# Joining the attention visits of units 8 to 11 on TensorE in a fused chunk-attention and MoE kernel

## The chip, the cores and the metric

The kernel runs on one core of one Trainium2 chip. The metric is the device time of one execution in microseconds (us). Before the change its median over 8 runs is 288.11 us, from 287.54 to 290.14.

## What is computed

`q`, `k` and `v` have shape (8, 8, 576, 64): 8 batches, 8 heads, 576 positions, 64 values per head, all in fp32. Attention is done inside chunks of 64 positions, with no mask. Its result, put together over the heads, is the 4608 x 512 input of a two-layer network with a gated activation.

```python
scores = (1/sqrt(64)) * q_c @ k_c.T          # per chunk of 64 positions, per head
attn   = softmax(scores)
x      = (attn @ v_c)                         # -> 4608 x 512, heads side by side
h      = x @ w_in                             # 512 -> 2048
out    = (h * sigmoid(beta * h)) @ w_out      # 2048 -> 512
```

## The kernel before, in words

**Tiles.** The 4608 tokens are cut into 18 units of 256 tokens. Two units make a block of 512 tokens, so there are 9 blocks, 0 to 8. A unit holds two halves of 128 tokens, called `s` = 0 and 1.

**Attention of one unit.** POOL (GpSimd) loads q and k in fp16 (L99 from unit 8 on, L105 before) and v into one large resident tile `vbig` (L113). From unit 8 on (`XU = 8`, L73) the q and k of a unit are turned by two DMA transposes that SP issues (`emit_T`, L152), first k and then q; before unit 8 VectorE does it. `emit_sc` then issues 32 matmuls of 64x64 (L225) that put the scores of the unit into the PSUM tile `s` (two banks), and one ScalarE exponential (L231) that writes `et`. `emit_pv` issues 32 matmuls of 64x65 (L266): for each half 16 products of `et` and v, with a column of ones that gives the row sums. `emit_norm` (L285, L287) takes reciprocals and multiplies on VectorE and leaves the half in `x16`. `emit_xt_dma` (L318) has SP issue the DMA transpose of that half into `xt`, the moving operand of the block's first layer.

**The network of one block.** `emit_m(j, m)` is one of 16 slices of the first layer: 4 matmuls of 128x128 by 512 (L329) into one PSUM bank `hps`, a tanh on ScalarE (L339) and a VectorE instruction (L343) that forms the gated slice. `emit_t(j, t)` is one of 4 tiles of 128 tokens of the second layer: 16 matmuls (L361), issued in two halves of 8, then a ScalarE copy out of PSUM (L371) and an output DMA on SP (L373). `hps`, `ops` and the tiles `y` (below) share four PSUM banks, the pool `ps_p`. The tiles `x` and `s` have two banks each.

**Order.** The order on each engine is the order in which the code emits, since the schedule is written out by hand. Blocks 0 to 2 are written out line by line. From block 3 on (L563) each block is a list of items sorted by a position between 0 and 1: the 16 slices `m` of block j, the 8 half tiles `t` of block j-1, and the attention of the two units of block j+1. An attention item between two items of the network makes TensorE leave its 128x128 matmuls for a set of 64x64 ones; I call that a visit.

**Two ways to place attention.** Units below `MU` = 12 (L74) get separate visits from `att_items` (L558): one for the scores (`sc`), and one for the second product (`pv`) 0.40 of a half block later. Their `pv` writes the halves 0 and 1 into the PSUM tiles `x` and `s`. From unit 12 on there is one visit per unit, a "hop" (L586): `pv` of unit u, right behind it the scores of unit u+1, then the DMA transposes of unit u+2, then the norms. A hop must leave the tile `s` to the scores, so its half 1, which is done first, goes into two `ps_p` banks as `y0` and `y1`, and half 0 into `x`. Hops stand at 0.22 and 0.68 of a block. At the end of block 4 a visit for the scores of unit 12 leads over to the hops.

**Queues.** SP issues output DMAs and all DMA transposes in order. POOL issues the loads in order. The load of a unit's q needs a buffer of the pool `qk` (4 deep), which comes free when the DMA transpose of the unit four before has landed. `emit_T(u)` also emits the loads up to unit u+4 (L164), except for units 6, 7 and 8.

Of the kernel before, what the change touches and what calls it, by code (L numbers as in the profile page):

```python
# [15 lines left out]
def kernel(  # L16
# [18 lines left out]
    NU = NT // UNIT  # L35
# [35 lines left out]
    blocks = [(u, 2) for u in range(0, NU, 2)]  # L71
    NB = len(blocks)
    XU = 8  # L73
    MU = 12  # L74
    unit_block = {}
    for j, (u0, n) in enumerate(blocks):
        for u in range(u0, u0 + n):
# [47 lines left out]
    def loads_to(u):  # L125
        while nxt[0] <= min(u, NU - 1):
            load_unit(nxt[0])
            nxt[0] += 1
# [16 lines left out]
    def emit_T(u, which=("kT", "qT")):  # L145
        for nm in which:
            src, dst = {"kT": (k_t, kT), "qT": (q_t, qT)}[nm]
            a = src.pop(u)
            t = qt_p.tile([128, H, CH, 2], FP16, tag=nm, name=nm)
            dst[u] = t  # L150
            if u >= XU:
                nc.sync.dma_start_transpose(  # L152
                    out=t.rearrange("p h s e -> p (h s e)").rearrange("p (j t) -> p j t", t=128),
                    in_=a.rearrange("p h r d -> p (h r d)"),
                )
                continue
            nc.vector.transpose(
                out=t.rearrange("p h s e -> p (h s e)").bitcast(FP32).rearrange(
                    "p (h i r) -> p h r i", h=H, r=2),
                in_=a.rearrange("p h r d -> p (h r d)").bitcast(FP32).rearrange(  # L160
                    "p (h r i) -> p h r i", h=H, r=2),
            )
        if which[-1] == "qT" and u not in (6, 7, 8):
            loads_to(u + 4)  # L164
# [48 lines left out]
    def emit_ex(u):  # L213
        ex_t[u].pop(0)()

    def emit_sc(u, split=False, later=False):
        qt, kt = qT.pop(u), kT.pop(u)
        sc = ps_s.tile([128, 2, H, CH], FP32, tag="s", name="sc")
        if u >= XU:
            qx, kx = (t.rearrange("p h s e -> p (h s e)").rearrange("p (j c t) -> p j c t", j=H, c=2)  # L220
                      for t in (qt, kt))
            for jj in range(H):
                for par in range(2):
                    for c in range(2):
                        nc.tensor.matmul(  # L225
                            out=sc[64 * c:64 * c + 64, par, jj, :],
                            lhsT=kx[64 * par:64 * par + 64, jj, c, :],
                            rhs=qx[64 * par:64 * par + 64, jj, c, :],
                        )
            et = et_p.tile([128, 2, H, CH], FP16, tag="et", name="et")  # L230
            nc.scalar.activation(out=et, in_=sc, func=ACTF.Exp, scale=scale)  # L231
            et_t[u] = et
            return
        for h in range(H):
            for e in range(2):
                for c in range(4):
                    p0, o0 = 32 * c, 64 * (c % 2)
                    nc.tensor.matmul(  # L238
                        out=sc[o0:o0 + 64, c // 2, h, :],
                        lhsT=kt[p0:p0 + 32, h, :, e],  # L240
                        rhs=qt[p0:p0 + 32, h, :, e],
                        start=(e == 0),
                        stop=(e == 1),
                    )
        et = et_p.tile([128, 2, H, CH], FP16, tag="et", name="et")
        ex_t[u] = [
            lambda s=s: nc.scalar.activation(out=et[:, s], in_=sc[:, s], func=ACTF.Exp, scale=scale)  # L247
            for s in ([0, 1] if split or later else [slice(0, 2)])
        ]
        et_t[u] = et  # L250
        while ex_t[u] and not later:
            emit_ex(u)

    def emit_pv(u, where=("x", "s")):
        et = et_t.pop(u)
        for s in (1, 0) if u >= MU else (0, 1):
            i = 2 * u + s
            if where[s] == "p":
                x = [ps_p.tile([128, 4, 128], FP32, tag="p", name=f"y{r}") for r in range(2)]
            else:  # L260
                pool = {"x": ps_x, "s": ps_s}[where[s]]
                x = [pool.tile([128, 2, 4, 128], FP32, tag=where[s], name="x")]
            for g in range(4):
                for r in range(2):
                    for c in range(2):
                        nc.tensor.matmul(  # L266
                            out=(x[0][64 * c:64 * c + 64, r, g, 0:D + 1] if len(x) == 1 else
                                 x[r][64 * c:64 * c + 64, g, 0:D + 1]),
                            lhsT=(et[64 * r:64 * r + 64, s, 4 * c + g, :] if u < XU else
                                  et[64 * r:64 * r + 64, g % 2, 4 * s + 2 * c + g // 2, :]),  # L270
                            rhs=vbig[64 * r:64 * r + 64, i, 4 * c + g, 0:D + 1],
                        )
            x_t[u, s] = x

    def emit_norms(u):
        for s in (1, 0) if u >= MU else (0, 1):
            emit_norm(u, s)
            emit_xt_dma(u, s)

    def emit_norm(u, s):  # L280
        x = x_t.pop((u, s))
        rd = rd_p.tile([128, 2, 4, 1], FP32, tag="rd", name="rd")
        x16 = x_p.tile([128, 2, 4, D], FP16, tag="x16", name="x16")
        for r, z in [(slice(0, 2), x[0])] if len(x) == 1 else list(enumerate(x)):
            nc.vector.reciprocal(out=rd[:, r], in_=z[..., D:D + 1])  # L285
            o = x16[:, r]
            nc.vector.tensor_tensor(  # L287
                out=o, in0=z[..., 0:D], in1=rd[:, r].to_broadcast(list(o.shape)), op=ALU.mult
            )
        x16_t[u, s] = x16  # L290

    def xt_at(u, s):
        j, o = unit_block[u]
        if j not in xt_t:
            xt_t[j] = xt_p.tile([128, 4, 4, 128], FP16, tag="xt", name="xt")
        return xt_t[j][:, 2 * o + s]
# [19 lines left out]
    def emit_xt_dma(u, s):  # L316
        xf = x16_t.pop((u, s)).rearrange("p r h d -> p (r h d)")
        nc.sync.dma_start_transpose(out=xt_at(u, s), in_=xf)  # L318
# [75 lines left out]
    with tc.manual_schedule():  # L394
# [74 lines left out]
        for i in range(16):  # L469
# [11 lines left out]
            if i == 15:  # L481
                a0, v0 = emit_m(1, 0, 0, 256, True)
# [46 lines left out]
        for m in range(KFF):  # L529
# [22 lines left out]
            if m == 7:  # L552
# [1 line left out]
                emit_gate(7)  # L554
                emit_xt_dma(7, 1)
                loads_to(11)

        def att_items(u, a0, w):  # L558
            return [(a0, 2, ("sc", u)), (a0 + 0.40 * w, 3, ("pv", u)),
                    (a0 + 0.40 * w, 4, ("norm", u, 0)), (a0 + 0.40 * w, 5, ("norm", u, 1)),  # L560
                    (a0 + 0.10 * w, 3, ("T", u + 1))]

        for j in range(3, NB):  # L563
            items = [(0.02 + 0.98 * m / KFF, 0, ("m", m)) for m in range(KFF)]
            for t in range(4):
                for hf in range(2):
                    items.append((0.98 * (t + 0.5 * hf) / 4, 1, ("t", t, hf)))
            if 2 * j + 2 < MU:
                for i in range(2):
                    items += att_items(2 * j + 2 + i, 0.03 + 0.43 * i, 0.43)  # L570
                if 2 * j + 4 == MU:
                    items += [(0.89, 2, ("sc", MU)), (0.90, 3, ("T", MU + 1))]
            elif j + 1 < NB:
                for i in range(2):
                    items.append((0.22 + 0.46 * i, 2, ("hop", 2 * j + 2 + i)))
            items.sort(key=lambda it: it[:2])
            for _, _, it in items:
                if it[0] == "m":
                    emit_m(j, it[1])
                elif it[0] == "t":  # L580
                    emit_t(j - 1, it[1], 8 * it[2], 8 * it[2] + 8)
                elif it[0] == "sc":
                    emit_sc(it[1])
                elif it[0] == "pv":
                    emit_pv(it[1])
                elif it[0] == "hop":  # L586
                    emit_pv(it[1], ("x", "p" if it[1] + 1 < NU else "s"))
                    if it[1] + 1 < NU:
                        emit_sc(it[1] + 1)
                    if it[1] + 2 < NU:  # L590
                        emit_T(it[1] + 2)
                    emit_norms(it[1])
                elif it[0] == "norm":
                    emit_norm(it[1], it[2])
                    emit_xt_dma(it[1], it[2])
                elif it[1] < NU:
                    emit_T(it[1])
        for t in range(3):
# [48 lines left out]
```

## Time and profile before

| what | value |
|---|---|
| median of 8 runs | 288.11 us |
| the profiled execution, its own time | 288.08 us |
| its span, first to last instruction | 286.2 us |
| PE busy | 278.9 us, 97% of the span |
| VectorE, ScalarE, POOL busy | 143.2, 146.5, 95.7 us |
| matmuls of L329 | 612, 136.3 us busy |
| matmuls of L361 | 560, 131.1 us busy |
| matmuls of L225 (scores, units 8 to 17) | 320, 32 in a visit |
| matmuls of L266 into `x` and into `y` | 464 and 112 recorded |
| DMA moved | 37.40 MB, mean 131 GB/s |
| granted TensorE clock | 1.000 |

The profile is of one execution. The span leaves 1.9 us of its own time outside. PE is TensorE's matmuls, PEld its weight loads, DVE VectorE, ACT ScalarE, SP the engine that issues DMAs. A line such as L329 is a line of the kernel. The chain of work follows from the last instruction back through what released each step; a stretch of it is a start, a length, and the instructions in it.

### The profile page before, as it was taken

To read this page: it belongs to the slowest core of one execution; us is meant where nothing else is said; L and a number is where in the kernel's file an instruction comes from. 1 tells how busy PE (TensorE), PEld (TensorE's weight loads), DVE (VectorE), ACT (ScalarE), POOL (GpSimd) and SP (SyncE) were. 2 spreads that over 40 slices of the span, in tenths; PEclk is the share of its full clock that TensorE was granted. 3 is DMA by queue.
4 is the path that set the end of the run, shared out by engine and by line. 5 is a ranking of instruction groups with operands and counts; after the bars stand their busy time and mean duration, and the time that the engine had idled before them with its cause. 6 is when DMAs were issued, how large, how long until landed. Compare 5 with 4: busy or idle time off the path is not lost.

```text
span 286.2 us, 6667 instructions
## 1 busy us (share of the span) xinstructions
PE 278.9 (97%) x2779; PEld 136.1 (48%) x2779; DVE 143.2 (50%) x264; ACT 146.5 (51%) x223; POOL 95.7 (33%) x125
## 2 busy tenths in 40 slices
PE   6889999999999999999999999999999999999995
PEld 3564456544544444444444444444444444444444
DVE  3678444776558553535353636354545544333301
ACT  4378228773557545454545555454546444444411
POOL 8753678488073991253643610000000000000000
PEclk9999999999999999999999999999999999999999
DMA  8999999999999999999999999364451212010012
GB/s 193 176 197 206 179 180 213 208 166 152 206 112 167 182 176 166 159 142 139 167 142 168 127 152 157 101 90 95 58 129 39 73 39 73 37 39 37 37 73 76
DMA packets 141085, 37.40 MB, mean 131 GB/s; under 512 B 128000, under 2 KB 136576, under 8 KB 141056
## 3 DMA queue, kind: packets, MB, share of 16 engines
q0 software_dynamic: 99136, 17.83, 80.5%
q1 hardware_dynamic: 41776, 19.09, 33.7%
q8 instruction: 22, 0.36, 0.5%
q10 hardware_dynamic: 144, 0.07, 0.1%
q14 instruction: 7, 0.06, 0.0%
HBM read 36.71 MB, written 9.44 MB: 161 GB/s over the span
## 4 chain that ended last, share of the span: by engine, by line
PE 94%; DMA 3%; ACT 1%; issue 1%; DVE 0%; POOL 0%; DVEq 0%; POOLq 0%
PE hps L329 44%; PE ops L361 43%; DMA h<-in_k_dram 3%; PE x L266 2%; PE sc L238 1%; PE ops L603 1%; PE sc L225 1%; ACT xt L304 1%; PE y L266 1%; PE xp L303 0%; PE sc L198 0%; ACT et L208 0%; POOL h L401 0%; PE warm L381 0%; PE xp L311 0%
## 5 line engine op out<-in xcount | busy, mean ns | idle before, releaser
L343 DVE SCALAR_TENSOR_TENSOR gt<-sg,hps 128x512 f16<-128x512 f32 (+1 forms) x153 | 99.2, 655 | 104.7 <-ACT sg L339 104.3
L339 ACT ACTIVATE sg<-hps,beta 128x512 f32<-128x512 f32 (+1 forms) x153 | 100.4, 663 | 71.9 <-PE hps L329 70.3
L329 PE MATMUL hps<-xt,win 128*128 128x512 f16 (+1 forms) x612 | 136.3, 367 | 0.8 <-ACT xt L304 0.7
L361 PE MATMUL ops<-wout,gt 128*128 128x512 f16 x560 | 131.1, 379 | 0.0
L329 PEld LDWEIGHTS <-win 128*128 128x128 f16 x612 | 58.4, 98 | 62.9 <-issue 0.9
L361 PEld LDWEIGHTS <-gt 128*128 128x128 f16 x560 | 53.8, 98 | 63.3
L371 ACT ACTIVATE osb<-ops 128x512 f32<-128x512 f32 x35 | 20.9, 598 | 42.6 <-PE ops L361 42.6
L113 POOL DMA_DIRECT2D vbig<-in_v_dram x40 | 34.1, 874 | 9.9 <-DMA wout<-in_moe_w_out_dram 3.7
L99 POOL DMA_DIRECT2D qu<-in_q_dram x22 | 18.7, 863 | 36.8 <-DMA qT<-qu 34.5
L287 DVE TENSOR_TENSOR x<-x,rd 128x512 f16<-128x512 f32 x29 | 20.1, 692 | 1.1
L99 POOL DMA_DIRECT2D ku<-in_k_dram x22 | 18.9, 880 | 0.2 <-issue 0.2
L285 DVE RECIPROCAL rd<-x 128x8 f32<-128x8 f32 x29 | 5.8, 199 | 12.4 <-PE x L266 12.4
L247 ACT ACTIVATE et<-sc 128x1024 f16<-128x1024 f32 (+1 forms) x8 | 6.4, 811 | 8.7 <-PE sc L238 8.7
L231 ACT ACTIVATE et<-sc 128x1024 f16<-128x1024 f32 x10 | 10.2, 1020 | 0.3
L266 PEld LDWEIGHTS <-et 64*64 64x64 f16 x576 | 6.0, 107 | 7.4 <-issue 3.8
L105 POOL DMA_DIRECT2D ku<-in_k_dram x9 | 6.8, 755 | 2.4 <-DMA win<-in_moe_w_in_dram 1.3
L381 PE MATMUL warm<-idle 128*128 128x512 f16 (+1 forms) x32 | 7.5, 385 | 0.0
L105 POOL DMA_DIRECT2D qu<-in_q_dram x9 | 6.8, 767 | 1.5 <-DMA win<-in_moe_w_in_dram 0.7
L266 PE MATMUL x<-vbig,et 64*64 64x65 f16 x464 | 7.0, 194 | 0.2 <-ACT et L208 0.2
L615 DVE TENSOR_SCALAR osb<-ops 128x256 f32<-128x256 f32 (+1 forms) x2 | 0.7, 358 | 12.1 <-PE ops L603 12.1
L131 POOL DMA_DIRECT2D win<-in_moe_w_in_dram x8 | 6.0, 756 | 1.7 <-DMA vbig<-in_v_dram 1.2
L179 DVE STREAM_TRANSPOSE t<-h 128x512 f32<-128x512 f32 (+1 forms) x5 | 4.4, 911 | 3.7 <-ACT h L178 3.2
(46 smaller groups left out, 75.2 us busy)
## 6 DMA issues: line engine op xcount, KB each, us to landing
out_dram<-osb SPq DMA_DIRECT2D x35, 256.0 KB, 3.4
vbig<-in_v_dram POOLq DMA_DIRECT2D x32, 128.0 KB, 7.6
qu<-in_q_dram POOLq DMA_DIRECT2D x20, 128.0 KB, 5.4
ku<-in_k_dram POOLq DMA_DIRECT2D x20, 128.0 KB, 6.5
win<-in_moe_w_in_dram POOLq DMA_DIRECT2D x8, 256.0 KB, 8.9
wout<-in_moe_w_out_dram POOLq DMA_DIRECT2D x4, 512.0 KB, 12.4
qu<-in_q_dram POOLq DMA_DIRECT2D x3, 256.0 KB, 7.3
ku<-in_k_dram POOLq DMA_DIRECT2D x3, 256.0 KB, 7.8
```

Source lines behind the costliest of these rows:

```text
L99: nc.gpsimd.dma_start(out=tv[off:off + n, sp], in_=src[b, :, s:s + n, :].rearrange("h p d -> p h d"),)
L105: nc.gpsimd.dma_start(out=t[off // 2:(off + n) // 2], in_=src[b, :, s:s + n, :].rearrange("h (p r) d -> p h r d", r=2),)
L113: nc.gpsimd.dma_start(out=vbig[off:off + n, i, :, 0:D], in_=v[b, :, s:s + n, :].rearrange("h p d -> p h d"),)
L231: nc.scalar.activation(out=et, in_=sc, func=ACTF.Exp, scale=scale)
L266: nc.tensor.matmul(out=(x[0][64 * c:64 * c + 64, r, g, 0:D + 1] if len(x) == 1 else x[r][64 * c:64 * c + 64, g, 0:D + 1]), lhsT=(et[64 * r ...
L287: nc.vector.tensor_tensor(out=o, in0=z[..., 0:D], in1=rd[:, r].to_broadcast(list(o.shape)), op=ALU.mult)
L329: nc.tensor.matmul(out=hps[:, 0:n], lhsT=w_in16[m // 2][:, kk, (m % 2) * 128:(m % 2) * 128 + 128], rhs=xr[:, c0 // CH:(c0 + n) // CH, 2 * ...
L339: nc.scalar.activation(out=sg[:, 0:n], in_=hps[:, 0:n], func=ACTF.Tanh, scale=beta2[:, m:m + 1])
L343: nc.vector.scalar_tensor_tensor(out=gt_t[j][:, m, c0:c0 + n], in0=sg[:, 0:n], scalar=1.0, in1=hps[:, 0:n], op0=ALU.add, op1=ALU.mult,)
L361: nc.tensor.matmul(out=ops, lhsT=gt_t[j][:, kk, t * 128:(t + 1) * 128], rhs=w_out16[kk // 4][:, kk % 4, :], start=(kk == 0), stop=(kk == K ...
L371: nc.scalar.activation(out=osb, in_=ops, func=ACTF.Copy, scale=0.5)
L381: nc.tensor.matmul(out=d[:, 0:w], lhsT=idle[:, 0:128], rhs=idle[:, 0:w])
```

## The change

`MU` becomes 8, so that units 8 to 11 are placed by hops as well, and `att_items` goes. The scores of unit 8, which no hop comes before, are issued in block 2 behind slice 14, and the DMA transposes of unit 9 behind slice 8 of block 2. In all blocks from 3 on the hops stand at 0.16 and 0.62 (in block 3 at 0.26 and 0.66), and the DMA transposes of unit u+2 are emitted 0.13 ahead of hop u and no longer inside it. The order of the halves, 1 before 0, and the place of half 1 in `y0` and `y1` now hold from unit 8 on.

```diff
-    MU = 12
+    MU = 8
...
+            if m == 8:
+                emit_T(9)
+            if m == 14:
+                emit_sc(8)
-
-        def att_items(u, a0, w):
-            return [(a0, 2, ("sc", u)), (a0 + 0.40 * w, 3, ("pv", u)),
-                    (a0 + 0.40 * w, 4, ("norm", u, 0)), (a0 + 0.40 * w, 5, ("norm", u, 1)),
-                    (a0 + 0.10 * w, 3, ("T", u + 1))]
...
-            if 2 * j + 2 < MU:
-                for i in range(2):
-                    items += att_items(2 * j + 2 + i, 0.03 + 0.43 * i, 0.43)
-                if 2 * j + 4 == MU:
-                    items += [(0.89, 2, ("sc", MU)), (0.90, 3, ("T", MU + 1))]
-            elif j + 1 < NB:
-                for i in range(2):
-                    items.append((0.22 + 0.46 * i, 2, ("hop", 2 * j + 2 + i)))
+            if j + 1 < NB:
+                for i, h in enumerate((0.26, 0.66) if j == 3 else (0.16, 0.62)):
+                    u = 2 * j + 2 + i
+                    items += [(h - 0.13, 3, ("T", u + 2)), (h, 2, ("hop", u))]
...
                 elif it[0] == "hop":
                     emit_pv(it[1], ("x", "p" if it[1] + 1 < NU else "s"))
                     if it[1] + 1 < NU:
                         emit_sc(it[1] + 1)
-                    if it[1] + 2 < NU:
-                        emit_T(it[1] + 2)
                     emit_norms(it[1])
```

The branches for the items `sc`, `pv` and `norm` go with `att_items`. The sorted items of blocks 3 and 4 (`t00` and `t01` are the two halves of tile 0; the norms, which issue nothing on TensorE, are left out):

```
block 3 before: t00 m0 sc8 T9 m1 t01 m2 pv8 m3 t10 m4 m5 t11 m6 m7 sc9 t20 T10 m8 m9 t21 pv9 m10 m11 t30 ...
block 3 after:  t00 m0 m1 t01 T10 m2 m3 t10 hop8 m4 m5 t11 m6 m7 t20 m8 T11 m9 t21 m10 hop9 m11 t30 ...
block 4 before: t00 m0 sc10 T11 m1 t01 m2 pv10 m3 t10 ... m7 sc11 t20 T12 m8 m9 t21 pv11 m10 ... m14 sc12 T13 m15
block 4 after:  t00 m0 T12 m1 t01 m2 hop10 m3 t10 ... m7 t20 T13 m8 m9 t21 hop11 m10 ... m15
```

More of the change, by code (lines that the diff above doesn't have):

```diff
@@ L581 @@
                     emit_t(j - 1, it[1], 8 * it[2], 8 * it[2] + 8)
[L582 to L585, printed above, removed]
                 elif it[0] == "hop":
@@ L589 @@
                         emit_sc(it[1] + 1)
-                    if it[1] + 2 < NU:
-                        emit_T(it[1] + 2)
                     emit_norms(it[1])
-                elif it[0] == "norm":
-                    emit_norm(it[1], it[2])
-                    emit_xt_dma(it[1], it[2])
                 elif it[1] < NU:
```

## The prediction

> **What bounds the kernel now.** I read the page first: which engine is busy, and whose work makes up the chain that ended last.
>
> ```profile
> PE 278.9 (97%) x2779; PEld 136.1 (48%) x2779; DVE 143.2 (50%) x264; ACT 146.5 (51%) x223; POOL 95.7 (33%) x125
> PEclk9999999999999999999999999999999999999999
> PE 94%; DMA 3%; ACT 1%; issue 1%; DVE 0%; POOL 0%; DVEq 0%; POOLq 0%
> ```
>
> TensorE is busy for 97% of the span and makes 94% of the chain, at full granted clock in every slice. VectorE and ScalarE are half idle. So a microsecond counts only if TensorE issues for a microsecond less, or stands still for one more.
>
> Second, the stages. I cut the span where the chain shows the first matmul of a block's `t00`, and added a stretch of block 8, which has no attention.
>
> ```profile
> 94.41:123.97 29.56, 29.56 (x258) 13.54 (x256) 14.20 (x25) 15.11 (x22) 17.18 (x21) 1.00 2.00 165
> 123.97:154.00 30.03, 30.03 (x289) 13.77 (x288) 14.69 (x25) 15.72 (x23) 13.42 (x17) 1.00 1.58 151
> 154.00:183.22 29.22, 29.22 (x258) 13.64 (x256) 14.09 (x29) 15.51 (x23) 5.26 (x6) 1.00 1.28 147
> 241.40:269.02 27.62, 27.62 (x129) 12.51 (x128) 11.00 (x17) 13.39 (x20) 0.00 (x0) 1.00 0.10 39
> ```
>
> The columns are the stretch, its length, then PE busy. TensorE has no gap in blocks 3, 4, 5 and 8. Without attention a block takes 27.62 us. Block 3, with four separate visits, takes 29.56; block 4, with five, 30.03; block 5, with two hops, 29.22.
>
> Third, the chain inside these blocks, for a separate visit and a hop, each between two slices `m`.
>
> ```profile
> 96.14 0.86 PE hps L329 x4
> 97.00 0.38 PE sc L225 x32
> 97.38 0.97 PE hps L329 x4
> ```
>
> ```profile
> 173.79 0.86 PE hps L329 x4
> 174.66 0.25 PE y L266 x16
> 174.91 0.13 PE x L266 x16
> 175.03 0.32 PE sc L225 x32
> 175.35 0.97 PE hps L329 x4
> ```
>
> A slice takes 0.86 us, but 0.97 behind a visit. The scores take 0.38 alone and 0.32 behind `pv`. So entering 64x64 matmuls costs about 0.06 and leaving them 0.10.
>
> **The change, part by part.**
>
> *Visits.* A separate visit costs (29.56 - 27.62) / 4 = 0.485 us by block 3, and (30.03 - 27.62) / 5 = 0.48 by block 4. A hop costs (29.22 - 27.62) / 2 = 0.80. Blocks 2 to 4 now have nine visits (`sc8` to `sc12`, `pv8` to `pv11`), 1.94 + 2.41 = 4.35 us. Afterwards they have one visit for `sc8`, 0.48, and four hops, 3.20: together 3.68. The difference is 0.67 us, all of it on the chain; by the lines of the chain (0.38 + 0.10, twice, less 0.80) it is 4 x 0.16 = 0.64. I take 0.65. The number of matmuls does not change, and blocks 5 to 7 keep their visits.
>
> The Trainium skill ("TensorE: Matmul & The Clock Gate", section "Wait — 56ns, not 53.3ns?") gives small matmuls a floor of about 25 ns from start to start. If that held here, a visit of 32 would take 0.8 us wherever it stands, joining two would save nothing, and the sum would be 0. The row disagrees: 32 matmuls in 0.38 us, 12 ns each.
>
> *PSUM.* The four new hops take two of the four `ps_p` banks for `y0` and `y1`. In the built order the nearest reuse is in block 3: `m5` takes the bank of `y0`, 0.80 + 0.86 = 1.66 us after the hop begins. In the trace VectorE's reciprocal and product of one `y` last 0.17 + 0.42, and they can begin about 0.4 after the hop's start, so the bank is free by about 1.1. The tile behind a hop (`t30` in block 3, `t10` from block 4 on) needs the bank of the slice just ahead of it. After the hop of 174.66 that slice's gated instruction ended 1.44 us after the hop began (first line below), and the tile began at 1.66 without waiting. So nothing, with 0.2 us of cover.
>
> *VectorE and ScalarE.* Half 1 in two pieces adds 2 x (0.17 + 0.42) - (0.20 + 0.69) = 0.29 us of VectorE per unit, hidden by an engine that is half idle. The exponentials keep their number, and the one of `sc8` stands ahead of the tanh of `m15` in block 2, whose result is needed only by `t01`, 3.5 us after `m15`.
>
> *DMA transposes of q and k.* T9 keeps its place on SP: before, it already left right behind the transposes of unit 7, at 91.27. T10 was emitted behind `sc9` and left at 108.62; now it follows the output DMA of 100.73, so k leaves at about 101.2 and q at 102.7, ahead of the two transposes of unit 8, which the new norms release at about 105 anyway. T11 follows the output of `t1`, at about 109 instead of 123.41, T12 at about 124 instead of 138.59. The scores come earlier too. q of unit 8 left at 82.75 and is needed at 93.45 (behind `m14` of block 2), q of 9 left at 93.22 and is needed at 103.9, q of 10 leaves at 102.7 and is needed at 115.9: they may take 10.7, 10.7 and 13.2 us. The longest landing of any q is 9.5. Nothing.
>
> *Loads.* POOL sits waiting for these transposes.
>
> ```profile
> 120.12 1.75 POOL L99 DMA_DIRECT2D qu<-in_q_dram  x2 [11.81 <-DMA qT<-qu]
> 133.79 2.27 POOL L99 DMA_DIRECT2D qu<-in_q_dram  x3 [8.43 <-DMA qT<-qu]
> ```
>
> These are the loads of units 14 and 15, released by T10 and T11. They now start near 112 and 120. No one needs the data sooner; what matters is what they collide with.
>
> *The transposes into `xt`.* Slice `m0` of block 4 needs all halves of units 8 and 9. Block 3 begins at 94.41 + 0.48 = 94.89. Ahead of `hop9` come six half tiles of 1.73, eleven slices of 0.86 and a hop of 0.80, so it begins at 115.55. Behind it follow its own 0.80, five slices (4.32) and three half tiles (5.18) before `m0`, which is due at 125.86. For the norms I use the hop at 174.66, which also stands directly behind a slice:
>
> ```profile
> 175.41 0.69 DVE L343 SCALAR_TENSOR_TENSOR gt<-sg,hps 128x512 f16<-128x512 f32 x1 [1.90 <-ACT sg L339]
> ...
> 176.78 0.42 DVE L287 TENSOR_TENSOR x<-y,rd 128x256 f16<-128x256 f32 x1
> ...
> 177.35 0.69 DVE L287 TENSOR_TENSOR x<-x,rd 128x512 f16<-128x512 f32 x1
> ```
>
> Half 1 is ready at 177.20, 2.54 us after its hop began. So SP can issue the first transpose of unit 9 at 118.1 and the second, one issue of 1.2 us later, at 119.3. That leaves 6.5 us for it to land. Before, `pv9` began at 114.85 with its norm straight behind it; the second was issued at 117.4 and had 8.2. How long these transposes take depends on what else moves:
>
> ```profile
> L318 SPq DMA_TRANSPOSE xt<-x x2: 1189/1203/1217, 116.1 to 117.4; - x2
> ...
> DMA to landing us min/median/max: 4.8/5.2/5.6
> ```
>
> ```profile
> L318 SPq DMA_TRANSPOSE xt<-x x2: 1217/1461/1705, 164.4 to 166.2; - x2
> ...
> DMA to landing us min/median/max: 7.6/8.0/8.5
> ```
>
> With no loads left (from 178 on) the slower of a pair takes 2.4 to 3.1. With loads under way there are eight pairs; their slower ones take 3.5, 4.4, 5.2, 5.4, 5.6, 6.1, 7.6 and 8.5. Six of eight land inside 6.5 us. The two others were issued while POOL was issuing loads. So this costs between 0 and 2.0 us; I take 0, as most rows do, and keep the 2.0 for the range. Unit 11 has more room: its hop stands directly behind a half tile, its second transpose leaves at about 147, and block 5 needs it at 155.
>
> A rule of the Trainium skill speaks against the change here: by "DMA: Bandwidth & Descriptors" (section "Issuing engines are not separate DMA queues") DMAs from all engines run on the same 16 DMA engines and interleave, so earlier loads slow these transposes. With equal turns for two queues 2.5 becomes about 5, an estimate, and the sum stays; the rows reach 8.5.
>
> **Sum.** 288.08 - 0.65 + 0 = 287.43 for the profiled execution, whose time lies 0.03 under the median of the runs. So 287.45 against 288.11, which is -0.23%.
>
> **The rivals.**
>
> 1. *The transposes of unit 9 land late* (slower). Place: `m0` of block 4, waiting for `xt`. For it: load 15 starts near 120, just behind the transposes, and load 14 is still landing, as in the pairs of 7.6 and 8.5. Against it: six pairs of eight. Price: 7.6 gives a stall of 1.1 and 288.5; 8.5 gives 2.0 and 289.4. It eats the gain from 7.15 on.
> 2. *Scores wait for their q or k.* TensorE would stop ahead of `sc8`, `sc9` or `sc10`. It needs a landing of over 10.7 us where the longest is 9.5; 12 us at one of them gives 288.7.
> 3. *It doesn't save what it says.* If the 0.10 and 0.06 at a visit's edges were covered by something else, or a wait inside the new hops took their place, the time stays at 288.1. Against it: all hops of blocks 5 and 6 cost the same 0.80 us.
>
> **How the numbers follow.** Forecast 0.62, around 287.45 with 0.3 either way for what runs scatter; rival 1 has 0.20, split evenly between 288.5 and 289.4; rival 2 0.08; rival 3 0.10. A measurement of this kernel can tell about 0.3%, 0.86 us, from no change: faster is below 287.25, slower above 288.97. The forecast lies 0.2 above the first bound, so I give 0.18 of its 0.62 to faster and 0.44 to the same. Rival 1 gives 0.10 to the same and 0.10 to slower, rival 2 gives 0.02 and 0.06, rival 3 its 0.10 to the same. Faster 0.18, same 0.66, slower 0.16. The range runs from 287.0, a little more than the whole gain, to 289.1, a stall of 1.7.
>
> **What the profile after would show.** Blocks 3 and 4 at 29.22 each, with four hops of 0.25, 0.13 and 0.32, and one `sc` of 0.38 near 93.5. Loads 14 and 15 starting near 112 and 120. TensorE without idle time at block 4's `m0`, and `xt` of unit 9 issued at 118.1 and 119.3 and landed by 125.9. A wait of L329 for a DMA near 126 would be rival 1, a wait of L225 rival 2; a longer slice behind `hop8` to `hop11`, or idle time of L361, would say that the PSUM step is wrong.

## The result, and the profile after

The changed kernel takes 290.71 us (median of 11 runs, 289.89 to 292.84) against 288.05 before (32 runs). The ratio is 1.010, with a 95% interval from 1.008 to 1.012: slower, outside the range of the prediction. The profiled execution took 289.89 us with a span of 287.8, 1.81 and 1.6 us more than before.

I read the page first, with the same three rows as before: busy time by engine, the granted clock, and the chain by engine; then the chain by line.

```profile
PE 278.6 (97%) x2779; PEld 136.3 (47%) x2779; DVE 144.3 (50%) x272; ACT 146.4 (51%) x223; POOL 95.6 (33%) x125
PEclk9999999999999999999999999999999999999999
...
PE 54%; DMA 3%; issue 1%; DVE 0%; DVEq 0%
PE ops L361 27%; PE hps L329 24%; DMA xt<-x 3%; PE ops L589 1%; PE sc L225 1%; PE y L266 1%; PE x L266 0%; DVE osb L601 0%; DVEq L601 0%
```

PE is busy for 0.3 us less (278.6 instead of 278.9), and its clock is full. But TensorE makes only 54% of the chain, where it made 94%: the chain is followed back only to a DMA into `xt`, which makes 3% of the span. The stages say where that is. The stretches are blocks 3, 4 and 5, cut at the first matmul of `t00` as before; the columns are the stretch, its length, and PE busy.

```profile
94.53:123.75 29.22, 29.22 (x258) 13.65 (x256) 14.19 (x29) 15.42 (x23) 18.11 (x22) 1.00 1.88 163
123.75:155.60 31.85, 29.40 (x258) 13.56 (x256) 14.68 (x29) 15.22 (x22) 15.73 (x20) 1.00 1.91 173
155.60:184.82 29.22, 29.22 (x257) 13.65 (x256) 14.67 (x29) 15.22 (x22) 1.53 (x2) 1.00 0.85 119
```

Block 3 went from 29.56 to 29.22, which is what the prediction wanted of it. Block 4 went from 30.03 to 31.85, and 31.85 - 29.40 = 2.45 us of it TensorE did nothing. The chain in order of time (start, length, what) names the place:

```profile
117.88 8.05 DMA xt<-x
125.93 2.00 issue
127.94 1.89 PE hps L329 x8
129.82 1.73 PE ops L361 x8
131.55 0.86 PE hps L329 x4
132.41 0.25 PE y L266 x16
132.66 0.13 PE x L266 x16
132.79 0.32 PE sc L225 x32
133.10 0.97 PE hps L329 x4
```

The slice `m0` of block 4 stands still until 127.94. The chain hangs it on the first transpose of unit 9, which landed at 125.93; the 2.00 us of "issue" behind it belong to the second, as its own tile shows (first line: the two issues, their durations in ns and their times; second: L329 waited for them once, for 2.5 us; third: the landings):

```profile
L318 SPq DMA_TRANSPOSE xt<-x x2: 1247/1250/1252, 117.9 to 119.2; - x2
...
  PE hps L329: 2.5, 1
...
DMA to landing us min/median/max: 8.1/8.3/8.6
```

119.2 + 8.6 = 127.8. The transposes left close to the times that the prediction gave (118.1 and 119.3). `m0` was due at 125.48, where the matmuls ahead of it ended (the prediction had 125.86). The transposes landed 8.1 and 8.6 us after their issue instead of within 6.5.

What stood ahead of them is in the queues of SP and POOL (start, duration, engine, operation):

```profile
100.87 1.48 SPq L152 DMA_TRANSPOSE kT<-ku  x1
102.46 3.97 SPq L152 DMA_TRANSPOSE qT<-qu  x1
106.52 3.80 SPq L318 DMA_TRANSPOSE xt<-x  x2
...
111.12 2.70 SPq L152 DMA_TRANSPOSE kT<-ku  x1
113.99 3.15 SPq L152 DMA_TRANSPOSE qT<-qu  x1
117.24 0.54 SPq L373 DMA_DIRECT2D out_dram<-osb  x1
117.88 2.59 SPq L318 DMA_TRANSPOSE xt<-x  x2
```

```profile
113.57 1.75 POOL L99 DMA_DIRECT2D qu<-in_q_dram  x2 [4.42 <-DMA qT<-qu]
...
125.43 0.87 POOL L99 DMA_DIRECT2D qu<-in_q_dram  x1 [1.97 <-DMA vbig<-in_v_dram]
```

T11 (k and q of unit 11) is issued from 111.12 to 117.1, right ahead of unit 9's transposes; its q takes 9.5 us and lands at 123.5. Load 14, released by the landing of T10's q, runs from 113.57 on. Before, T11 left SP at 123.41 and load 14 began at 120.12 (the POOL line in the prediction), both behind these transposes:

```profile
116.12 2.50 SPq L318 DMA_TRANSPOSE xt<-x  x2
122.90 0.33 SPq L373 DMA_DIRECT2D out_dram<-osb  x1
123.41 1.49 SPq L152 DMA_TRANSPOSE kT<-ku  x1
```

**One measure for all runs.** The first blocks differ by some tenths between executions. So for each profile I take the time from the first matmul of the visit `pv7` in block 2 to the end of the last matmul. Before this is 282.92 - 86.95 = 195.97 us. Behind the change it is 197.88, +1.91: -0.66 for the joined visits (measured below), +2.45 of idle time, and +0.16 for the first group behind the gap (`m0` and `m1`), which takes 1.89 in the chain where such a group takes 1.73 without a gap; together 1.95.

The time outside the span (time of a run less its span) differs as well. It is 2.06 to 2.25 us in the runs of the changed kernel and of the experiments built on it, and 1.73 to 1.92 in the runs of the kernel before beside the experiments and of e3 and e8, which are built on that one. These 0.3 us are in the ratios below and not in the fixed point; no run shows where they come from.

### The profile page after: what moved, and what is told of

Its sections match the earlier page's. It is cut to its first block, busy times and chain, and to the rows that moved or that the text cites. A ratio compares the mean times of both kernels' runs of the same rounds, so it can differ in the third digit from the quotient of the medians.

```text
span 287.8 us, 6675 instructions
## 1 busy us (share of the span) xinstructions
PE 278.6 (97%) x2779; PEld 136.3 (47%) x2779; DVE 144.3 (50%) x272; ACT 146.4 (51%) x223; POOL 95.6 (33%) x125
## 4 chain that ended last, share of the span: by engine, by line
PE 54%; DMA 3%; issue 1%; DVE 0%; DVEq 0%
PE ops L361 27%; PE hps L329 24%; DMA xt<-x 3%; PE ops L589 1%; PE sc L225 1%; PE y L266 1%; PE x L266 0%; DVE osb L601 0%; DVEq L601 0%
## 5 line engine op out<-in xcount | busy, mean ns | idle before, releaser
L343 DVE SCALAR_TENSOR_TENSOR gt<-sg,hps 128x512 f16<-128x512 f32 (+1 forms) x153 | 99.2, 655 | 103.6 <-ACT sg L339 102.8
L329 PE MATMUL hps<-xt,win 128*128 128x512 f16 (+1 forms) x612 | 136.0, 367 | 3.3 <-issue 2.5
L329 PEld LDWEIGHTS <-win 128*128 128x128 f16 x612 | 58.2, 98 | 65.4 <-issue 3.7
L287 DVE TENSOR_TENSOR x<-x,rd 128x512 f16<-128x512 f32 x25 | 17.3, 692 | 1.0
L285 DVE RECIPROCAL rd<-x 128x8 f32<-128x8 f32 x25 | 5.0, 199 | 11.4 <-PE x L266 11.4
L287 DVE TENSOR_TENSOR x<-y,rd 128x256 f16<-128x256 f32 x22 | 9.3, 424 | 0.8
```

Source lines behind the costliest of these rows:

```text
L287: nc.vector.tensor_tensor(out=o, in0=z[..., 0:D], in1=rd[:, r].to_broadcast(list(o.shape)), op=ALU.mult)
L329: nc.tensor.matmul(out=hps[:, 0:n], lhsT=w_in16[m // 2][:, kk, (m % 2) * 128:(m % 2) * 128 + 128], rhs=xr[:, c0 // CH:(c0 + n) // CH, 2 * ...
L343: nc.vector.scalar_tensor_tensor(out=gt_t[j][:, m, c0:c0 + n], in0=sg[:, 0:n], scalar=1.0, in1=hps[:, 0:n], op0=ALU.add, op1=ALU.mult,)
```

## The experiments

The result left two candidates for the slow landing, T11 ahead of the transposes (theory B) and load 14 beside them (theory A), and one for the gap that would not be a landing at all: that joined visits themselves bring it. Kernels with four inserted lines ahead of the same code number it 4 higher, so L333, L322 and L347 there are L329, L318 and L343 here. The ratios are against the kernel before, run beside them on the same chip. The last three columns, in us, come from one profiled execution each: the change at the fixed point, the slower of the two transposes of unit 9 into `xt`, and the idle time of TensorE at `m0` of block 4.

| run | what is early (ahead of unit 9's transposes) | ratio, 95% | fixed point | slower landing | idle at `m0` |
|---|---|---|---|---|---|
| changed | T11 and load 14 | 1.010 [1.008, 1.012] | +1.91 | 8.6 | 2.45 |
| e1 | T11 | 1.0042 [1.002, 1.0063] | +0.05 | 6.7 | 0.23 |
| e2 | load 14 | 1.008 [1.0063, 1.0097] | +2.51 | 8.3 | 1.92 |
| e3 | both, visits separate | 1.0072 [1.0052, 1.0092] | +1.86 | 8.2 | 1.72 |
| e4 | both, hop earlier | 1.0133 [1.0114, 1.0152] | +3.98 | 8.4 | 2.79 |
| e5 | T11 | 1.0063 [1.0038, 1.0089] | -0.16 | 7.0 | 0.31 |
| e6 | neither | 1.0021 [1.0005, 1.0037] | +0.18 | 4.9 | 0 |
| e7 | T11, still earlier | 1.0039 [1.0008, 1.0071] | +0.63 | 7.0 | 1.10 |
| e8 | T11, and load 14 just ahead; visits separate | 1.0072 [1.0056, 1.0089] | +1.94 | 8.2 | 1.82 |
| e9 | neither | 0.9984 [0.9969, 0.9998] | -0.66 | 3.9 | 0 |
| e10 | neither, T13 late too | 0.9988 [0.9973, 1.0003] | -0.69 | 4.5 | 0 |
| e11 | T11 and load 14 (changed kernel again) | 1.0122 [1.0081, 1.0163] | +1.28 | 8.1 | 1.76 |
| e12 | T11 and load 14 (changed kernel, one run) | - | +1.88 | 8.6 | 2.41 |

The three profiles of the changed kernel add up in the same way: -0.66, the wait and 0.16 give 1.95, 1.26 and 1.91, and the fixed point gives 1.91, 1.28 and 1.88.

### e1: loads 14 and 15 behind unit 9

```diff
-        if which[-1] == "qT" and u not in (6, 7, 8):
+        if which[-1] == "qT" and u not in (6, 7, 8, 10, 11):
...
+            if (u, s) == (9, 0):
+                nc.gpsimd.tensor_copy(out=gate, in_=x16_t[u, s][:, 0, 0, 0:1])
...
+        if u == 9:
+            loads_to(15)
```

POOL copies one element of unit 9's second norm before it loads unit 14, so the loads cannot start earlier.

> The changed kernel, with one POOL instruction more: the loads of units 14 and 15 wait for the norms of unit 9 (a one-element copy out of that half, as the kernel already has for units 6 and 7), so they start near 119 and not at 113.6. The early transposes T10 and T11 stay. Theory A (the loads released earlier fill the 16 DMA engines while the transposes of unit 9 into xt are under way): the second of them lands in 6 us or less where the changed kernel took 8.6, TensorE does not stand still ahead of m0 of block 4, and the time is 287.4 (-0.65 against the kernel before). Rival B (it is T11, issued by the same queue just ahead of them): they still take 7.5 us or more, a stall of 1 to 3 us stays, and the time is 288.5 to 290.7.

Measured: 289.3 us against 288.46, still slower. Load 14 began at 120.28, the transposes landed after 6.5 and 6.7 us:

```profile
L322 SPq DMA_TRANSPOSE xt<-x x2: 1217/1218/1218, 118.9 to 120.2; - x2
...
DMA to landing us min/median/max: 6.5/6.6/6.7
```

Nearly 2 us less landing, and 0.23 of idle time left at block 4, 0.15 at block 5 (unit 11's transposes now took 8.6). So load 14 is a part of the cause, and not all: with T11 alone ahead it still takes 6.7. The profiled execution is only 0.05 over the kernel before at the fixed point, the median of the runs 0.8. Of that, 0.3 lies outside the span; the rest isn't explained by one profile.

### e2: T11 behind unit 9

```diff
-                for i, h in enumerate((0.26, 0.66) if j == 3 else (0.16, 0.62)):
+                for i, h in enumerate({3: (0.26, 0.66), 4: (0.30, 0.62)}.get(j, (0.16, 0.62))):
...
-                    items += [(h - 0.13, 3, ("T", u + 2)), (h, 2, ("hop", u))]
+                    items += [(h + 0.001 if u == 9 else h - 0.13, 3, ("T", u + 2)), (h, 2, ("hop", u))]
```

T11 goes behind the transposes of unit 9, and `hop10` from 0.16 to 0.30, since its scores need T11.

> The changed kernel, with T11 issued behind the transposes of unit 9 and not ahead of them, so that load 15 follows later too; hop 10 moves to 0.30 of block 4 so that its scores do not wait for T11. Load 14 stays early. Theory A: load 14 alone still crowds, the second transpose of unit 9 takes 7 to 8.5 us, the time is 288.5 to 290. Rival B: with T11 out of the way it lands in 6 us or less, and the time is 287.4.

Measured: 291.06 us, no better than the change. The transposes take 7.3 and 8.3 us with no T11 ahead of them:

```profile
L318 SPq DMA_TRANSPOSE xt<-x x2: 1192/1720/2249, 118.4 to 119.7; - x2
...
DMA to landing us min/median/max: 7.3/7.8/8.3
```

That is against B alone, as e1 is against A alone. Another 0.81 us of idle time stands behind the moved hop, where `m` waits for a PSUM bank (it shows again in e6).

### e3: the kernel before, with only T10 and T11 moved

```diff
-                    items += att_items(2 * j + 2 + i, 0.03 + 0.43 * i, 0.43)
+                    items += [it for it in att_items(2 * j + 2 + i, 0.03 + 0.43 * i, 0.43)
+                              if it[2] not in (("T", 10), ("T", 11))]
+                if j == 3:
+                    items += [(0.13, 3, ("T", 10)), (0.53, 3, ("T", 11))]
```

No visit is joined; two items of block 3 stand where the change puts them.

> The kernel before with its separate visits, and only T10 and T11 moved to the places that the change gives them, which releases loads 14 and 15 early. Theories A and B: the slower transpose of unit 9 takes about 8 us instead of 5.6; it is issued 1.8 us earlier than in the changed kernel, so the stall is 0 to 1 us and the time 288.1 to 289.1. Rival C (the moved transposes and loads are harmless, and the hop itself is late with its norms): it takes 4.8 to 5.6 us as before, no stall, 288.05.

Measured: 290.49 us, 1.86 more at the fixed point. TensorE idles at `m0` of block 4 as in the changed kernel:

```profile
127.08 1.02 PE L329 MATMUL hps<-xt,win 128*128 128x512 f16 x4 [1.72 <-issue]
```

So the loss needs no joined visit: the moved transposes of q and k alone bring it. I had expected unit 9's transposes to leave earlier than in the changed kernel, since `pv9` stands earlier here. They didn't, and SP's queue shows why:

```profile
110.83 2.61 SPq L152 DMA_TRANSPOSE kT<-ku  x1
113.61 3.27 SPq L152 DMA_TRANSPOSE qT<-qu  x1
116.99 0.55 SPq L373 DMA_DIRECT2D out_dram<-osb  x1
117.64 3.67 SPq L318 DMA_TRANSPOSE xt<-x  x2
```

The norms were ready at 115.75 and 116.65. SP was still issuing T11: k and q took 2.61 and 3.27 us to issue, where T12 later took 1.29 and 1.24 in e6. So T11 does harm twice, as traffic and as a late issue.

### e4: hop 9 earlier

```diff
-                for i, h in enumerate((0.26, 0.66) if j == 3 else (0.16, 0.62)):
+                for i, h in enumerate((0.26, 0.62) if j == 3 else (0.16, 0.62)):
```

> The changed kernel with the second hop of block 3 at 0.62 instead of 0.66: one slice earlier, and no longer directly behind a slice, so that the transposes of unit 9 can be issued about 1.7 us earlier, near 116.2 and 117.4. If their time to land is a fixed 8.6 us, the stall of the profiled run falls from 2.5 to about 0.6 us and the time to about 288.5 (rival C, too little time, would be most of it). If they land when the DMA engines have worked off what is ahead of them, whenever they were issued (theory A), they land near 127 again, and the time stays above 289.5.

Measured: 292.63 us, the slowest of all. Counted from the fixed point, `hop9` began 0.86 us earlier, as intended (27.67 instead of 28.53), and its norms were ready at 116.60 and 117.50. But SP issued T11 from 111.95 to 118.45 and an output behind it, so the transposes left at 119.20, which is 0.5 later than in the changed kernel (31.81 from the fixed point instead of 31.29). So the run doesn't show what an earlier issue is worth. `m0` then waits 2.79 us, and something new follows. These are four stretches of 2 us, the first inside the wait; the number behind POOL's busy time is the mean granted clock.

```profile
127.00:129.00 2.00, 0.00 (x0) 0.00 (x0) 0.00 (x0) 0.00 (x0) 0.65 (x1) 1.00 1.58 223
129.00:131.00 2.00, 1.93 (x7) 0.87 (x8) 0.04 (x1) 0.69 (x1) 0.68 (x1) 0.71 1.56 158
131.00:133.00 2.00, 2.00 (x7) 0.62 (x6) 0.98 (x2) 0.69 (x1) 0.88 (x1) 0.50 1.72 156
133.00:135.00 2.00, 2.00 (x10) 0.82 (x8) 0.36 (x1) 0.59 (x1) 0.68 (x1) 0.94 1.83 155
```

```profile
129.07 2.84 PE L329 MATMUL hps<-xt,win 128*128 128x512 f16 x8 [2.79 <-issue]
131.71 2.66 PE L361 MATMUL ops<-wout,gt 128*128 128x512 f16 x8
```

The clock falls to 0.50 for some 2 us, and two groups of 1.89 take 2.84 and 2.66. Of the 3.98 us, -0.66 is the visits, 2.79 the wait, and the rest, 1.85, comes behind it: 0.95 + 0.77 = 1.72 in these two groups. All four runs of e4 have a mean granted clock of 0.992 or 0.993.

### e5, e6, e7: loads 14 to 16 gated, T11 in three places

All three gate the load of unit u+5 on unit u's norm, for u = 9, 10 and 11, as e1 does for unit 9:

```diff
+        if which[-1] == "qT" and u not in (6, 7, 8) and not 10 <= u <= 13:
...
+            if 9 <= u <= 11 and s == 0:
+                nc.gpsimd.tensor_copy(out=gate, in_=x16_t[u, s][:, 0, 0, 0:1])
...
+        if 9 <= u <= 11:
+            loads_to(u + 5)
```

e5 is this alone. e6 adds the edit of e2 (T11 behind unit 9, `hop10` at 0.30). e7 issues T11 inside `hop8`, ahead of unit 8's transposes:

```diff
+                    items += [(h - 0.13, 3, ("T", u + 2))][:u != 9] + [(h, 2, ("hop", u))]
...
                     if it[1] + 1 < NU:
                         emit_sc(it[1] + 1)
+                    if it[1] == 8:
+                        emit_T(11)
```

> The changed kernel, with the loads of units 14, 15 and 16 each held until the norms of unit 9, 10 and 11 (three one-element POOL copies), so that they come about one per 13.5 us as in the kernel before. Where the first gate alone left two small stalls (0.23 us at block 4, where the slower transpose of unit 9 took 6.7 us, and 0.15 us at block 5, where that of unit 11 took 8.6), theory A expects the second to go, since load 15 to 17 no longer bunch ahead of it: unit 11 lands in about 5 us, and the time is 0.2 to 0.4 us under the kernel before. If T11 to T13 and not the loads fill the engines (rival B), unit 11 still takes over 8 us and the time stays 0 to 0.5% above.

Measured: 289.73 us against 288.17, with runs from 288.2 to 292.18. Its profile is the fastest of the twelve runs of this kernel: 7.0 us for unit 9's transposes, 0.31 of idle time, nothing at block 5, where unit 11's took 6.8, between the 5 of theory A and the 8 of rival B. The profile shows that the gate works there; it doesn't show why the other runs are slower. The three slowest (291.06 to 292.18) have a mean granted clock of 0.992 to 0.994, like the runs of e4, the others 0.998 or more. A landing of 7 us with no slack, and in those three a long wait, is my guess, no more.

> The same gates, and T11 behind the transposes of unit 9 with hop 10 at 0.30 of block 4. With neither load 14 nor T11 ahead of them the transposes of unit 9 have the engines to themselves: 3 to 5 us, no stall at block 4, under theory A and under rival B alike. If hop 10 finds its q in time (it left 0.8 us of idle time at 137.5 behind hop 10 in the run without gates, for a bank), the time is 0.65 us under the kernel before; with those 0.8 us it is level.

Measured: 288.56 us. With both away, the transposes land after 3.4 and 4.9 us, well inside 6.5:

```profile
L322 SPq DMA_TRANSPOSE xt<-x x2: 1189/1506/1822, 118.1 to 119.4; - x2
...
DMA to landing us min/median/max: 3.4/4.2/4.9
```

Nothing waits at `m0`. The gain is lost again at the moved `hop10`:

```profile
135.10 1.02 PE L333 MATMUL hps<-xt,win 128*128 128x512 f16 x4 [0.80 <-DVE gt L347]
```

At 0.30 the hop follows a slice, and another slice comes right behind it. That one needs the bank of the slice ahead of the hop, whose gated instruction was not yet done. This is the wait that the prediction watched for at the change's own hops, and which isn't found there, with `hop10` at 0.16; at 0.30 it comes.

> The same gates, and T11 issued right behind the scores of unit 9 inside hop 8, ahead of the transposes of unit 8, so about 106.5 and not 111. It then has 11 us to land before the transposes of unit 9 are issued, and SP is free when their norms are done. Theory A with T11 as the second part of it: the slower one lands in 5 us, no stall, and the time is 0.65 us under the kernel before (287.4). If the engines are behind by then whatever the order, it takes 6.5 us or more and the time is level with before.

Measured: 289.43 us. I expected no wait at `m0`; it waited 1.10 us. Unit 8's transposes left only at 113.98, behind T11, and two outputs behind them held unit 9's until 118.11, where the norm was ready at 117.66. Unit 9's still took 7.0. Making T11 still earlier doesn't get it out of the way.

### e8: e3 with loads 14 and 15 gated

```diff
-        if which[-1] == "qT" and u not in (6, 7, 8):
+        if which[-1] == "qT" and u not in (6, 7, 8, 10, 11):
...
+                    if it[1:] == (9, 1):
+                        nc.gpsimd.tensor_copy(out=gate, in_=x16_t[9, 1][:, 0, 0, 0:1])
                     emit_xt_dma(it[1], it[2])
+                    if it[1:] == (9, 1):
+                        loads_to(15)
```

Added to e3's edit; here half 1 is the second norm.

> The kernel before with separate visits and the early T10 and T11 (which alone cost 1.7 us of idle time at block 4), and the loads of units 14 and 15 held until the norms of unit 9. Theory A: the slower transpose of unit 9 falls from 8.2 to 6.5 us or less and the idle time goes, time as before (288.1). Rival B (T11 in front on SP): it stays near 8 us, 1 to 2 us slower than before.

Measured: 290.13 us, with landings of 7.9 and 8.2: the gate brought nothing. But it isn't the clean test of T11 that I wanted. The gate opened at 117.64, load 14 left at 118.14, and SP, busy with T11 from 111.96 to 118.0 and an output, issued unit 9's transposes only at 118.73. The load was ahead of them after all. With both ahead its 8.2 agrees with e3's; on T11's share the run says nothing.

### e9, e10: both away, the hop where no bank is missing

e9 is e6 with `hop10` at 0.26. e10 does the same one block later: T13 behind unit 11, `hop12` at 0.26.

```diff
-                for i, h in enumerate((0.26, 0.66) if j == 3 else (0.16, 0.62)):
+                for i, h in enumerate({3: (0.26, 0.66), 4: (0.26, 0.62), 5: (0.26, 0.62)}.get(j, (0.16, 0.62))):
...
-                    items += [(h - 0.13, 3, ("T", u + 2)), (h, 2, ("hop", u))]
+                    items += [(h + 0.001 if u in (9, 11) else h - 0.13, 3, ("T", u + 2)), (h, 2, ("hop", u))]
```

The lines are those of e10; e9 leaves out `5: (0.26, 0.62)` and has `u == 9`.

> The gated kernel with T11 behind the transposes of unit 9, and hop 10 at 0.26 of block 4 instead of 0.30, behind a half tile and not behind a slice whose bank is wanted at once. The present theory: any one of two things that the change moved ahead of the transposes of unit 9, the early load 14 or the early T11, is enough to make them take 7 us or more; with both away they took 4.9. So no idle time at block 4, and the 0.8 us of idle time behind hop 10 goes: four visits fewer are left, 0.65 us under the kernel before (287.4 beside 288.05). If the earlier run's remaining loss lay elsewhere, it stays level with before. T11 must land before the scores of hop 10, near 133; it landed at 131.6.

Measured: 287.75 us against 288.23 beside it. The landings of unit 9, and blocks 3 and 4:

```profile
L322 SPq DMA_TRANSPOSE xt<-x x2: 1190/1337/1484, 118.3 to 119.5; - x2
...
DMA to landing us min/median/max: 3.6/3.7/3.9
```

```profile
95.03:124.26 29.23, 29.23 (x258) 13.65 (x256) 14.20 (x29) 15.40 (x23) 17.57 (x23) 1.00 1.90 169
124.26:153.48 29.22, 29.22 (x257) 13.67 (x256) 14.86 (x29) 15.21 (x22) 14.23 (x20) 1.00 1.70 161
```

TensorE is busy in all of both blocks, and the fixed point gives -0.66. The transposes leave hardly earlier than in the changed kernel (23.24 us behind the start of block 3, there 23.35), so it is the landing that differs. Load 14 starts at 119.70 and T11 at 121.21, just behind the transposes and beside their landing; that does them little harm (3.9 us, against 2.4 to 3.1 with no loads left). What counts is what is queued or under way ahead of them. T10 is as early here as in the change, so T10 as traffic has no part in the loss; its landing is only what releases load 14 early there.

> As the run with hop 10 at 0.26, and T13 moved in the same way behind the transposes of unit 11, with hop 12 at 0.26 of block 5. In the gated run the slower transpose of unit 11 took 7.9 us and landed about 0.4 us ahead of its use, so some executions should have waited there. Expected: it lands in about 5 us, the scatter of the runs shrinks, and the median is 0.65 us or a little more under the kernel before.

Measured: 287.61 us, -0.69 at the fixed point, unit 11's transposes 5.2 us where e1 had 8.6. The scatter did not shrink (287.26 to 288.82, in e9 287.51 to 288.33). I expected 0.65 us less in both; the medians of the spans, 285.6 and 285.5 beside 286.35, are 0.75 and 0.85 shorter, and 0.3 of that is lost outside the span. Both lie 0.1 to 0.2% under the kernel before; the interval of e9 ends just under 1, that of e10 just above, so this gain is at the edge of what can be told.

### e11, e12: the changed kernel again

No edit.

> The changed kernel once more, unaltered, beside the two others on the same chip. Expected as before: about 1% slower, the slower transpose of unit 9 at 8 us or more, and runs in two groups, near 290 and near 292. The run with the longest stall so far (2.8 us) showed the granted clock at 0.50 for some 2 us behind it; if this profile falls in the upper group, it shows the same.

> One more profile of the changed kernel, for the two groups of its times. Near 290 us it should show, like the two profiles so far, 1.8 to 2.5 us of idle time at block 4 and a granted clock of 1.00 throughout. Near 292 us it should show 2.7 us or more and the clock at about 0.5 for 2 to 3 us behind it; if it is near 292 and the clock stays at 1.00, the second group has another cause.

Measured: 291.69 us (289.33 to 293.01) in e11, where e9 and e10 ran on the same chip, and 290.21 in e12. The landings were 8.1 and 8.6 us, the idle times at `m0` 1.76 and 2.41, the clock full in both. The runs of the changed kernel lie in two groups: ten from 289.33 to 290.91, with a mean granted clock of 0.998 to 1.000, and nine from 291.51 to 293.01, with 0.992 to 0.994. So a lower clock goes with the upper group, of the size that e4's profile shows (0.993). The profiles caught only the lower group. That a longer wait sets off the fall, as in e4, is argued and not shown.

## Why the prediction was wrong, step by step

- **Visits: right.** -0.65 was predicted. Block 3 takes the predicted 29.22, and with nothing else in the way e9 and e10 measure -0.66 and -0.69 for the whole. By the Trainium skill's floor of about 25 ns ("TensorE: Matmul & The Clock Gate", section "Wait — 56ns, not 53.3ns?"), weighed there, it would have been 0, an estimate; the runs stand with the 12 ns of the row.
- **PSUM, VectorE and ScalarE: right.** No idle time stands behind the change's own hops. That the cover was thin, as its 0.2 us said, shows in e2 and e6: `hop10` moved to 0.30 waits 0.8.
- **Transposes of q and k: times nearly right, "Nothing" right for their own readers only.** T10 left at 100.87 and 102.46 (predicted 101.2 and 102.7), T11 at 111.12 instead of 109, behind unit 8's transposes, whose two issues had stretched to 3.80 together. No scores waited. The step asked only whether T10 and T11 come in time for the scores, not what stands behind them on SP.
- **Loads: right for load 14, not for load 15.** Load 14 began at 113.57 (112 predicted), load 15 only at 125.43 (120), when the first transpose of unit 9 was landing.
- **The transposes into `xt`: the step that failed.** Issue (117.88 and 119.2) and due time (125.48) were nearly right; they leave 6.3 us where 6.5 was predicted. The landing was taken as "inside 6.5 us", at a cost of 0, because six of eight pairs did so. It took 8.6, and the wait 2.45. The change put T11 and load 14 directly ahead of just this pair, as the working itself had found two steps earlier, and the eight rows were no fair draw for that. Sorted by what stood ahead, the rows of before pointed to the answer. The pair of 8.5 left SP right behind T14 and beside load 16, the situation of the change:

```profile
160.34 1.29 SPq L152 DMA_TRANSPOSE kT<-ku  x1
161.73 2.62 SPq L152 DMA_TRANSPOSE qT<-qu  x1
164.44 3.01 SPq L318 DMA_TRANSPOSE xt<-x  x2
```

```profile
160.11 1.76 POOL L99 DMA_DIRECT2D qu<-in_q_dram  x2 [7.53 <-DMA qT<-qu]
...
163.57 1.81 POOL L113 DMA_DIRECT2D vbig<-in_v_dram  x2
```

The pair of 7.6 (103.25) had loads beside it and no T issued since 95.1; unit 9's own pair of 5.6 (116.12) had T10 ahead of it and no load issued since 108.3. The sorting is rough: the pairs at 65.3 and 88.5 had loads near them too and took 6.1 and 5.4. With 8.6 the sum is 288.08 - 0.65 + 2.45 + 0.16 = 290.04, and the profile says 289.89; its first blocks were 0.36 shorter and its time outside the span 0.2 longer.
- **Rival 1 was what happened**, with its place and nearly its price. Its longest row, 8.5, was nearly the landing. Its upper end of 2.0 was too low because only 6.3 us were left and the matmuls started 0.1 behind the landing. The waits seen in the changed kernel are 1.76 to 2.45, in e4 2.79 with a clock at half behind it.
- **The time outside the span: a term that the sum doesn't have.** The sum starts from the time before and takes off what TensorE saves, as if the rest stayed. With the change 0.3 us more lie outside the span, so even with nothing in the way about half of the 0.65 doesn't reach the time (e9: 287.75 against 288.23).
- **The cause** is T11 and load 14 together. With both ahead the landing is 8.1 to 8.6 (e8 counted here), with one of them 6.7 to 8.3, with neither 3.9 to 4.9. Neither theory held alone. Unit 8's transposes, with T10 and loads ahead of them, took up to 8.6 in the changed kernel and up to 8.5 in e9 as well; they have the time. How much each has by itself isn't settled: e1 says that the load is worth 1.9 us, e2 that T11 is worth nearly nothing, e6 that without the load T11 is worth 2.1 (7.0 in e5 against 4.9). The two don't add up.

The rule of the Trainium skill weighed there, that DMAs of all engines interleave on the same 16 DMA engines ("DMA: Bandwidth & Descriptors", section "Issuing engines are not separate DMA queues"), agrees with these runs: the same two transposes take 3.9 to 8.6 us by what SP and POOL had issued ahead. The estimate of 5 us for two equal queues was too low: with load 14 alone ahead it was 8.3 (e2), with T11 alone 6.7 to 7.0 (e1, e5, e7).

## What to carry to other kernels

When a change moves a DMA, ask two things: whether its own reader gets it in time, and which transfers that somebody else waits for now stand behind it, on the issuing queue and on the DMA engines. For a transfer with little slack, take the landing from rows with the same traffic ahead, not the share of all rows that happen to fit. Here the joined visits were worth 0.66 us and the transposes moved along with them cost 2.6. The 0.66 came back inside the span when q, k and loads followed the transposes that TensorE was waiting for; in the time of the whole execution it is 0.5 to 0.6, at the edge of what can be told.

## What the runs showed of the hardware

- Behind an idle time of TensorE of 2.79 us the granted clock fell to 0.71, 0.50 and 0.94 in successive stretches of 2 us (e4). Behind 2.45, 2.41, 1.92 and 1.82 it stayed at full in the profiles of the changed kernel, e12, e2 and e8. The Trainium skill ("TensorE: Matmul & The Clock Gate", section "What's actually happening") gives half clock after at least one idle window of about 3.4 us, a window that runs freely. The half agrees with the 0.50; the gap here was shorter than 3.4. What sets the fall off isn't tested.
- Issuing a DMA isn't of fixed length. Issuing the transpose of one unit's q on SP took 1.24 us for unit 12 in e6 and 3.97 for unit 10 in the changed kernel (at 102.46), and everything behind it on SP waits.
- The same pair of transposes lands after 3.9 us (e9) or 8.6 (the changed kernel, e12), and a load and a T started right behind it (e9) did it little harm.
